# A shared accumulator tile of two banks is closed and made anew as two tiles of one bank each

## The chip, the cores and the metric

The kernel runs on one core of one Trainium2 chip. The metric is device time in microseconds of one execution, as a median of runs. TensorE (PE) multiplies, with its weight loads listed as PEld; VectorE (DVE), ScalarE (ACT) and GpSimd (POOL) do the elementwise work; SyncE (SP) issues the transfers. Products are summed in PSUM, eight banks of 512 fp32 numbers per partition, from which DVE and ACT read them.

## The reference, cut to what matters

Linear attention with positive random features, 8 batches of 8 heads, 576 tokens, head width 64, 128 features, and behind it a two-layer network on 4608 tokens of width 512, hidden width 2048:

```python
def phi(x):
    h = x @ omega.T - sum(x * x) / 2
    return exp(h - max(h)) / sqrt(m)
q_p, k_p = phi(q * scale), phi(k * scale)
kv, z = k_p.T @ v, sum(k_p)
x = (q_p @ kv) / (q_p @ z + 1e-06)          # heads side by side: 4608 x 512
h = x @ w_in                                 # 512 -> 2048
out = maximum(0.01 * h, h) @ w_out           # 2048 -> 512
```

## The kernel before

Nearly every operand is split into two fp16 parts, and a product is three passes of matmuls (high by high, high by low, low by high). The tokens go through in nine blocks of 512 (`NB`), counted by `j`. For each block `query_block` makes the attention's output (features by the matmuls of line 609, numerators by those of lines 899 to 901) and `feed_forward` applies the two layers. `key_batch` makes the keys' sums. For the first two blocks `first_layer` (line 1048) does the first layer in plain products. From block 2 on (`FIRST_FAST`), `fast_first_layer` takes a Strassen-like scheme of seven products in place of eight (line 1102), whose partial sums are read out of PSUM and combined by ACT and DVE. The second layer is plain (line 1284) up to block 6, and by seven products (line 1209) from block 7 on (`TAIL`).

The class `Plan` collects all operations with estimated durations, walks through them with a greedy list scheduler, and emits them in the order found; each engine's queue then holds that order. The order is fixed when the program is built, and on the chip an engine only waits for semaphores. A recording layer under the kernel adds these semaphore waits from who reads and who writes each tile.

PSUM's eight banks are given out as `pj` (two banks, for projections), `pj0` (two banks, a second one for the first phase), `ffn` (three tiles of a bank) and `mi` (one bank), in line 298. `pj0` is needed by class `Whole` alone, for the first two key batches and the first query block (line 688). Afterwards its halves serve as the places 3 and 4 of the kind `ffn`: lines 306 to 309 append two views of the one tile to `tiles["ffn"]`, and `over` tells the planner that they come free only when every buffer of the kind `pj0` has been used up. So from then on a buffer of the kind `ffn` may lie in one of three tiles of its own, or in either half of a fourth tile of two banks. The function `at` (line 369) maps a planned buffer to its tile. In the profile a name such as `pj<-xt,w` at line 1102, 1048, 1284 or 1209 is one of these halves; `pj` at line 609 is the projection's own tile.

In `four_tiles` the buffers `a`, `c` and `d` of a quadrant are such places (lines 1148 to 1171): `product(a, ...)` fills `a`, `so_far(a)` reads it by ACT or DVE (line 360 is the helper behind it), `product(d, ...)` fills another, `add(u1, d)` reads it by DVE (line 1118), and then `product(a, "S2", ...)` goes on adding into `a`, for which it has to wait until `so_far(a)` has read it. In the plain first layer each result is read by an ACT activation (line 1057), in the plain second layer by line 360.

In the built program before, waits on `pj0` are by the whole tile: a read of one half waits for the last matmul that stands ahead of it in the planned order into either half, and a matmul into one half waits for the reads of both.

Of the kernel before, what the change touches and what calls it, by code (L numbers as in the profile page):

```python
# [8 lines left out]
F32 = mybir.dt.float32  # L9
# [6 lines left out]
PSUM = bass.MemoryType.PSUM  # L16

P = 128
# [248 lines left out]
def performer_ffn(ctx: ExitStack, tc, qT, kT, qn, kn, vn, omT, eye, w_in, w_out, out):  # L267
# [3 lines left out]
    ps = ctx.enter_context(tc.tile_pool(name="ps", bufs=1, space=PSUM))  # L271
# [26 lines left out]
    banks = {"pj": (1, 1024), "pj0": (1, 1024), "ffn": (3, 512), "mi": (1, 512)}  # L298
    tiles = {k: [sb.tile(shape, dt, tag=f"{k}{i}", name=f"{k}_{i}") for i in range(n)]
             for k, (n, shape, dt) in kinds.items()}  # L300
    for k, (n, size) in banks.items():
        tiles[k] = [ps.tile([P, size], F32, tag=f"{k}{i}", name=f"{k}_{i}") for i in range(n)]
    scratch = tiles["mi"][0][:, 384:]


    over = {}
    for i in range(2):
        over["ffn", len(tiles["ffn"])] = [("pj0", 0)]
        tiles["ffn"].append(tiles["pj0"][0][:, 512 * i:512 * i + 512])
    late = tiles["v1"][0].rearrange("p g e -> p (g e)")  # L310
    half = HP * VT * E
    tiles["vr"] = [late[:, :half].rearrange("p (g e) -> p g e", e=E)]
# [54 lines left out]
                     for e, c, g in (("POOL", pool_(n), nc.gpsimd), ("DVE", stt(n), nc.vector)) if e in engines], **of)  # L367

    def at(b):
        return tiles[b.kind][b.place]  # L370

    def flat(a):
# [38 lines left out]

    whole = buf("xt")
    om32 = lambda: at(whole).rearrange("p i c t -> p (i c t)").bitcast(F32)[:, :2 * M]
    minus_half = lambda: at(whole).rearrange("p i c t -> p (i c t)").bitcast(F32)[:, 2 * M:4 * M]

    def omega():
# [29 lines left out]
    class Weight:  # L446
# [12 lines left out]
        def load(self, i, prio):  # L459
            w, b = self.w, buf("big")  # L460
            self.raws[i] = b

            def run():
                raw = at(b).bitcast(U32)
                if self.name == "w1":
                    k, s = i % 4, i // 4
                    nc.sync.dma_start(out=raw, in_=w[k * P:(k + 1) * P, 2048 * s:2048 * (s + 1)])
                else:
                    nc.sync.dma_start(out=raw.rearrange("p (f e) -> p f e", e=2 * DM),
                                      in_=w[2 * i * P:2 * (i + 1) * P, :].rearrange("(f p) x -> p f x", p=P))  # L470
            op("SP", 0.45, run, w=[b], prio=prio, moved=1 << 20)
# [915 lines left out]
```

## Time and profile before

| | us |
|---|---|
| median of 3 runs | 942.38 |
| lowest and highest run | 939.09 and 943.46 |
| the profiled execution: its own time | 938.46 |
| the profiled execution: span of its instructions | 936.7 |
| PE busy | 886.2 (95%) |
| DVE busy | 752.0 (80%) |
| ACT busy | 606.9 (65%) |
| POOL busy | 326.5 (35%) |

The span is the time from the first to the last instruction of the profiled execution; 1.8 us of its own time lie around it. Up to about 140 us weights are converted and the first attention blocks made; from then on matmuls of the network and of the attention alternate on PE. A matmul's duration in the profile is longer than the distance to the next, since they are pipelined: matmuls of 256 columns that take 273 ns follow each other every 109 ns, those of 512 columns that take 379 ns every 216 ns.

### The profile page before, as it was taken

The numbers are of one execution on the slowest core, as the hardware profiler recorded it, in microseconds if no ns is written. First come the engines' busy times: TensorE is split into PE (matmuls) and PEld (weight loads), VectorE is DVE, ScalarE is ACT, GpSimd is POOL, SyncE is SP. The second block draws the span as 40 slices with busy tenths as digits, with TensorE's granted clock in tenths as the row PEclk, the third lists the DMA queues.
The fourth block names the chain that finished last, engine by engine and source line by source line (L and its number), as shares of the span: only waits on it lengthen the run. The fifth ranks groups of instructions, "written<-read, shape, count | busy, mean of one in ns | idle before, by whom it ended". The sixth has DMA issues, their size and how long they took to land.

```text
span 936.7 us, 20382 instructions
## 1 busy us (share of the span) xinstructions
PE 886.2 (95%) x8102; PEld 633.8 (68%) x8102; DVE 752.0 (80%) x1384; ACT 606.9 (65%) x905; POOL 326.5 (35%) x290
## 2 busy tenths in 40 slices
PE   4786999999999799999999999999999999998998
PEld 3774566555455685588557855786579657887887
DVE  7999788988888689887778887877988788992861
ACT  5786795567665587578756864686568555653741
POOL 2333637567745344125211531172115222210010
PEclk7897999999999999999999999999999999999999
DMA  9798236975489998788789997888698886632401
GB/s 366 282 258 252 56 60 136 238 191 120 94 187 274 275 236 195 188 210 244 156 183 243 233 219 187 203 236 181 115 237 215 196 158 162 178 77 88 135 1 45
DMA packets 279103, 171.17 MB, mean 183 GB/s; under 512 B 195296, under 2 KB 242144, under 8 KB 277984
## 3 DMA queue, kind: packets, MB, share of 16 engines
q1 hardware_dynamic: 279008, 169.87, 71.9%
q8 instruction: 63, 1.03, 0.5%
q14 instruction: 32, 0.26, 0.1%
HBM read 105.87 MB, written 16.78 MB: 131 GB/s over the span
## 4 chain that ended last, share of the span: by engine, by line
PE 82%; DVE 8%; DMA 4%; ACT 3%; issue 2%; SPq 1%; DVEq 0%; ACTq 0%
PE ffn L1284 16%; PE ffn L1102 14%; PE pj L1284 12%; PE pj L1102 10%; PE ffn L1048 6%; PE pj L609 5%; PE ffn L1209 5%; PE pj L1209 3%; PE pj L688 2%; PE pj L1048 2%; DMA xt<-xn 1%; DMA t<-z 1%; PE mi L899 1%; DVE wt L487 1%; PE mi L806 1%
## 5 line engine op out<-in xcount | busy, mean ns | idle before, releaser
L1102 PEld LDWEIGHTS <-w 128*128 128x128 f16 x2352 | 228.4, 98 | 42.2 <-issue 11.5
L366 POOL TENSOR_TENSOR big<-row,big 128x512 f16<-128x512 f32 x116 | 148.5, 1292 | 272.5 <-ACT big L360 261.8
L1284 PEld LDWEIGHTS <-big 128*128 128x128 f16 x1344 | 127.3, 98 | 136.3
L1284 PE MATMUL ffn<-wt,big 128*128 128x512 f16 x816 | 190.2, 379 | 0.0
L1102 PE MATMUL ffn<-xt,w 128*128 128x256 f16 x1044 | 140.8, 274 | 3.3 <-DMA xt<-xn 3.1
L1284 PE MATMUL pj<-wt,big 128*128 128x512 f16 x528 | 124.1, 379 | 0.0
L640 ACT ACTIVATE p<-p,little 128x1024 f32<-128x1024 f32 x68 | 70.0, 1029 | 52.9 <-DVE p L637 52.9
L617 DVE TENSOR_REDUCE st<-pj 128x8 f32<-128x1024 f32 x68 | 73.1, 1075 | 25.7 <-PE pj L609 25.4
L1102 PE MATMUL pj<-xt,w 128*128 128x256 f16 x660 | 93.1, 273 | 0.5 <-ACT row L360 0.5
L1048 PE MATMUL ffn<-xt,w 128*128 128x512 f16 x312 | 73.6, 387 | 8.3 <-DMA xt<-xn 7.9
L360 ACT ACTIVATE big<-row 128x512 f16<-128x512 f32 x128 | 77.1, 621 | 3.0 <-DVE row L1074 2.3
L366 DVE TENSOR_TENSOR ph<-p,ph 128x1024 f16<-128x1024 f32 x56 | 72.6, 1296 | 6.8 <-ACT ph L360 6.6
L637 DVE SCALAR_TENSOR_TENSOR p<-pj,sc,st 128x1024 f32<-128x1024 f32 x68 | 77.1, 1134 | 0.7
L569 ACT ACTIVATE z<-nat 128x512 f32<-128x512 f32 (+1 forms) x56 | 36.3, 648 | 55.2 <-DMA t<-z 44.8
L1048 PEld LDWEIGHTS <-w 128*128 128x128 f16 x384 | 37.0, 99 | 50.6 <-issue 11.7
L609 PE MATMUL pj<-om,t 128*128 128x128 f16 x944 | 64.0, 219 | 4.2 <-DMA t<-z 2.4
L609 PEld LDWEIGHTS <-t 128*128 128x128 f16 x944 | 57.7, 98 | 14.6 <-DMA t<-z 3.7
L1102 PE MATMUL ffn<-w,w 128*128 128x256 f16 x360 | 58.9, 272 | 1.7 <-ACT z L1229 1.7
L360 ACT ACTIVATE ph<-p 128x1024 f16<-128x1024 f32 x56 | 58.8, 1050 | 0.7
L366 POOL TENSOR_TENSOR v<-xp,v 128x768 f16<-128x768 f32 (+1 forms) x15 | 26.5, 1768 | 86.5 <-ACT v L360 86.4
L571 DVE TENSOR_REDUCE sq<-z 128x8 f32<-128x512 f32 (+1 forms) x56 | 39.6, 708 | 18.5 <-ACT z L569 18.4
L1125 ACT ACTIVATE row<-row 128x512 f32<-128x512 f32 x71 | 43.8, 623 | 14.2 <-DVE row L1118 13.8
(236 smaller groups left out, 1804.5 us busy)
## 6 DMA issues: line engine op xcount, KB each, us to landing
w<-w1d SPq DMA_DIRECT2D x196, 256.0 KB, 3.3
v<-vn SPq DMA_DIRECT2D x28, 650.0 KB, 4.8
big<-w_in SPq DMA_DIRECT2D x8, 1024.0 KB, 9.8
big<-w_out SPq DMA_DIRECT2D x8, 1024.0 KB, 6.0
nat<-qn SPq DMA_DIRECT2D x32, 256.0 KB, 3.7
out<-row SPq DMA_DIRECT2D x32, 256.0 KB, 2.7
w1d<-wt SPq DMA_DIRECT2D x16, 256.0 KB, 3.2
nat<-kn SPq DMA_DIRECT2D x12, 320.0 KB, 3.8
```

Of the source, the lines that this page charges most:

```text
L360: ("ACT", act(n, int(pointer)), lambda: nc.scalar.activation(dst(), src(), AF.Copy, scale=1.0 if scale is None else value()), False),
L366: return ways([(e, c, lambda g=g: g.tensor_tensor(dst(), a(), b(), op=ALU.subtract), True) for e, c, g in (("POOL", pool_(n), nc.gpsimd), ...
L571: op("DVE", dve(n), lambda: nc.vector.tensor_reduce(at(self.sq)[:, :2 * nt], square().rearrange("p (g d) -> p g d", d=D), axis=AX.X, op=AL ...
L609: nc.tensor.matmul(at(pj)[:, 512 * h + c * M:512 * h + (c + 1) * M], at(self.t)[:, 2 * (c0 + c) + h, :], om[:, w, :], start=(w == 0), stop ...
L617: op("DVE", dve(n * M), lambda: nc.vector.tensor_reduce(row(0), pv(), axis=AX.X, op=ALU.max), r=[pj], w=[st], prio=prio)
L637: op("DVE", dve(n * M), lambda: nc.vector.scalar_tensor_tensor(p(), pv(), down(), row(2).rearrange("p (g o) -> p g o", o=1).broadcast_to([ ...
L640: op("ACT", act(n * M, 1), lambda: nc.scalar.activation(flat(p()), flat(p()), AF.Exp, bias=shift), w=[p32], r=["ones"], prio=prio)
L1048: nc.tensor.matmul(at(ph), wk[wp][:, c:c + P], xt[:, 512 * xp:512 * xp + 512], start=(i == 0), stop=(i == 3 * KT - 1))
L1102: nc.tensor.matmul(pair(bank)[:, f], wt[:, k, wp, f * P:f * P + P], operand(xname, k, xp), start=(first and f == k == i == 0), stop=(k == ...
L1125: op("ACT", act(512), lambda: nc.scalar.activation(at(g), at(src), AF.Prelu, scale=H_DOWN * (TAIL_DOWN if tail else 1.0), alpha=0.01), r=[ ...
L1209: nc.tensor.matmul(pair(bank)[:, t], g()[:, gp, f, t * P:t * P + P], operand(wname, 2 * q + f, wp), start=(first and q == t == f == i == 0 ...
L1284: nc.tensor.matmul(at(po), g_(q)[:, s, gp, t * P:(t + 1) * P], wf[wp], start=(q == s == 0 and gp == wp), stop=(q == s == 3 and gp == 1))
```

## The change

`pj0` is taken from a pool of its own. The two extra places of the kind `ffn` stay empty at first. The first time that `at` is asked for one of them, while the planned order is being emitted, that pool is closed, which gives its two banks back, and a new pool with two tiles of one bank each is opened there; the places now hold these. The planner gets the same kinds, places and rules.

```diff
+    first = ExitStack()
     for k, (n, size) in banks.items():
-        tiles[k] = [ps.tile([P, size], F32, tag=f"{k}{i}", name=f"{k}_{i}") for i in range(n)]
+        pool = first.enter_context(tc.tile_pool(name="ps0", bufs=1, space=PSUM)) if k == "pj0" else ps
+        tiles[k] = [pool.tile([P, size], F32, tag=f"{k}{i}", name=f"{k}_{i}") for i in range(n)]
...
         over["ffn", len(tiles["ffn"])] = [("pj0", 0)]
-        tiles["ffn"].append(tiles["pj0"][0][:, 512 * i:512 * i + 512])
+        tiles["ffn"].append(None)
+
+    def two_banks():
+
+        first.close()
+        ps2 = ctx.enter_context(tc.tile_pool(name="ps2", bufs=1, space=PSUM))
+        for i, place in enumerate(p for p, tile_ in enumerate(tiles["ffn"]) if tile_ is None):
+            tiles["ffn"][place] = ps2.tile([P, 512], F32, tag=f"late{i}", name=f"late_{i}")
...
     def at(b):
+        if tiles[b.kind][b.place] is None:
+            two_banks()
         return tiles[b.kind][b.place]
```

Each engine's queue holds the same instructions with the same shapes in the same order as before. Of the 1788 matmuls that went into a half of `pj0` after 140 us, each now goes into a tile `late_0` or `late_1`. The tiles lie in other banks than before (`pj0` was in banks 2 and 3 and its successors are in 6 and 7; `ffn` moved from 4 to 6 to 2 to 4, and `mi` from 7 to 5). What differs besides is the waits. Of the 108 reads by ACT and DVE out of the former halves, 34 wait for an earlier matmul than before, 6 to 84 matmuls earlier in PE's order, and three name one 12 matmuls later, a matmul that an earlier wait of the other reader used to stand for. On PE some 60 waits of matmuls for ACT or DVE fall away, name an earlier read, or move to a matmul further on. There is one new wait: the first matmul into `late_0` (at 143.29 us in the trace before) waits for PE's own 574th matmul, the last of line 688 into `pj0` (118.41 us). POOL's and SP's queues have the same waits.

## Rows read from the trace of the kernel before

**Rows 1.** The page: busy time by engine, then the chain that ended last, shares by engine.
```profile
PE 886.2 (95%) x8102; PEld 633.8 (68%) x8102; DVE 752.0 (80%) x1384; ACT 606.9 (65%) x905; POOL 326.5 (35%) x290
...
PE 82%; DVE 8%; DMA 4%; ACT 3%; issue 2%; SPq 1%; DVEq 0%; ACTq 0%
```

**Rows 2.** Waits of PE, 140 to 937: who waited for whom, total us, times, longest.
```profile
PE pj L1102 <- ACT row L360: 3.4, 6, 0.7
PE ffn L1102 <- DMA xt<-xn: 3.1, 1, 3.1
PE pj L609 <- DMA t<-z: 2.4, 2, 1.9
PE mi L901 <- DMA qp<-ph: 2.2, 1, 2.2
```

**Rows 3.** Timeline, 419 to 449: start, us, engine, line, operation, count, [idle before <-releaser].
```profile
421.91 0.49 PE L1102 MATMUL pj<-xt,w 128*128 128x256 f16 x3
422.50 0.60 ACT L360 ACTIVATE row<-pj 128x512 f32<-128x512 f32 x1 [1.82 <-PE pj L1102]
...
423.15 0.49 PE L1102 MATMUL pj<-w,w 128*128 128x256 f16 x3 [0.74 <-ACT row L360]
...
443.23 0.60 ACT L360 ACTIVATE row<-pj 128x512 f32<-128x512 f32 x1 [1.14 <-PE pj L1284]
...
443.88 0.49 PE L1102 MATMUL pj<-w,w 128*128 128x256 f16 x3 [0.74 <-ACT row L360]
...
447.61 0.49 PE L1102 MATMUL pj<-w,w 128*128 128x256 f16 x3 [0.75 <-ACT row L360]
```

**Rows 4.** Timeline, six later places where PE restarts, and one reader.
```profile
501.84 0.49 PE L1102 MATMUL ffn<-xt,w 128*128 128x256 f16 x3 [0.15 <-ACT row L360]
...
606.34 0.92 PE L1102 MATMUL pj<-xt,w 128*128 128x256 f16 x7 [0.32 <-ACT row L360]
...
696.57 0.60 PE L1102 MATMUL pj<-xt,w 128*128 128x256 f16 x4 [0.18 <-ACT row L360]
...
794.59 0.49 PE L1102 MATMUL pj<-w,w 128*128 128x256 f16 x3 [0.21 <-DVE z L1118]
...
803.51 0.49 PE L1102 MATMUL pj<-w,w 128*128 128x256 f16 x3 [0.89 <-DVE row L1118]
...
860.60 0.60 ACT L360 ACTIVATE row<-pj 128x512 f32<-128x512 f32 x1 [2.95 <-PE pj L1209]
861.25 0.49 PE L1102 MATMUL pj<-w,w 128*128 128x256 f16 x3 [0.69 <-ACT row L360]
```

**Rows 5.** Timeline, 233 to 270: a chain through three engines, and a read like its first.
```profile
233.88 2.75 PE L1048 MATMUL pj<-xt,w 128*128 128x512 f16 x12
...
236.67 0.60 ACT L1057 ACTIVATE row<-pj 128x512 f32<-128x512 f32 x1 [1.81 <-PE pj L1048]
...
238.48 0.69 DVE L571 TENSOR_REDUCE sq<-z 128x8 f32<-128x512 f32 x1 [1.00 <-ACT z L569]
...
249.61 0.38 PE L609 MATMUL pj<-om,t 128*128 128x128 f16 x4 [1.75 <-DVE p L637]
...
269.56 0.69 ACT L360 ACTIVATE row<-pj,s 128x512 f32<-128x512 f32 x1 [3.92 <-PE pj L1284]
```

**Rows 6.** The chain in order of time, 200 to 330: one transfer, start, us.
```profile
285.96 7.74 DMA t<-z
```

**Rows 7.** Busy us by stretch: PE, PEld, DVE, ACT, POOL, then PEclk, DMA share, GB/s.
```profile
275.00:300.00 25.00, 23.07 (x189) 12.39 (x188) 23.32 (x41) 12.76 (x17) 14.10 (x13) 1.00 0.98 266
322.70:326.10 3.40, 3.40 (x20) 2.48 (x18) 2.83 (x3) 2.95 (x4) 1.39 (x2) 0.50 0.79 264
420.00:450.00 30.00, 27.76 (x299) 23.57 (x298) 21.34 (x43) 23.55 (x41) 17.25 (x14) 1.00 0.83 226
780.00:803.00 23.00, 22.40 (x209) 18.60 (x207) 21.55 (x34) 15.36 (x27) 7.20 (x4) 1.00 0.60 164
```

**Rows 8.** The page, DMA issues: count, KB each, median us from issue to landing.
```profile
t<-z SPq DMA_TRANSPOSE x56, 3.5
```

## The prediction

> **What bounds the kernel now.** I read the page first: PE is busy for 95% of the span, and 82% of the chain that ended last runs through it [rows 1]. Then the view of waits, from 140 us on, where the change acts. PE waits there for little, and the four rows that I keep are most of it: 3.4 us for ACT reads of a half of the shared tile, in six places, and 3.1 + 2.4 + 2.2 = 7.7 us for transfers [rows 2]. So PE sets the end. A gain counts only if it takes a stall out of PE's queue, and it can hardly be more than the stalls that are there. The timeline then shows what a stall costs and who ends it. At 421.91 PE starts its last three matmuls into one half of the tile. ACT has been idle for 1.82 us and begins to read the other half only at 422.50, when these matmuls are through; PE goes on at 423.15, when ACT has read [rows 3]. The half that ACT reads was complete before, since 12 matmuls into the other half, at a pitch of 0.109 us, stand in between. So the two halves take turns here though they are two banks.
>
> The Trainium skill, Perfetto Trace Analysis, section Matmuls, says that independent matmul groups should rotate through different PSUM banks, so that ACT or DVE read one while the next group runs. By that rule alone the kernel before has what the change brings and the sum would be nothing; the row at 422.50 disagrees, since its read waits 1.82 us although the banks differ.
>
> **What one stall costs.** The idle time that the view prints is counted from the modelled end of the last matmul, and understates it. At 421.91 the three matmuls start at 421.91, 422.02 and 422.13; the next would start at 422.24 and starts at 423.15, so 0.91 us are lost where the view prints 0.74. The difference of about 0.16 is the duration of 0.27 less the pitch of 0.11; for 512 columns it is 0.379 less 0.216, the same. I add 0.16 to each printed idle time.
>
> **The change part by part.** The order on all engines stays, so no instruction and no transfer is added. The new wait of PE for its own 574th matmul is 25 us late (118.41 against 143.29) and costs nothing; a few extra semaphore instructions on ACT and DVE stand in place of others that go. The other banks have no price in any row; I take 0. What is left is the waits.
>
> *Three places at 423, 444 and 448.* ACT's read no longer waits for the other half. At 422.50 ACT could have read 1.82 us earlier: read done at about 421.3, PE wants the half at 422.24, cover 0.95 us. At 443.23 ACT was idle for 1.14, so the read ends at about 442.7 and PE wants it at about 443.0: cover 0.3 us. The third is like it [rows 3]. All three stalls go whole: 0.90 + 0.90 + 0.91 = 2.7 us. If ACT were busier there, as after PE has moved, up to 0.6 each could come back; that is the lower bound, 0.9 us.
>
> *606, 697 and 861.* The same figure: 0.32 + 0.16 = 0.48, 0.18 + 0.16 = 0.34, 0.69 + 0.16 = 0.85 [rows 4]. At 860.60 ACT had been idle for 2.95 us, so its read has room. Sum 1.7 us, bounds 0.8 and 1.7.
>
> *502.* PE waits for a read of another tile that stands in ACT's queue behind a read of a half: 0.15 + 0.16 = 0.3 us [rows 4], bounds 0 and 0.3, and I take 0.2, since another matmul's wait comes close behind.
>
> *795 and 804.* The matmul at 794.59 waits for a DVE read of the other half and loses 0.37 us [rows 4]; this wait goes. But at 803.51 PE waits for DVE's read of its own half, which stays, and DVE is busy for 21.55 of the 23 us ahead of it [rows 7]. A PE that comes 0.37 earlier waits 0.37 longer. I take 0 for the pair.
>
> *250.* From 233.88 twelve matmuls, six into one half and six into the other, and ACT reads the first six only at 236.67 after an idle time of 1.81. With the change it may read six pitches of 0.216, so 1.3 us, earlier. Behind it in ACT's queue stands the square for which DVE sits idle 1.00 us, and DVE is then gapless up to the operation for which PE waits at 249.61, printed as 1.75 [rows 5]. DVE's idle time is the cap: 1.0 us, bounds 0 and 1.0.
>
> *294.* The same figure recurs at 269.56, where ACT reads a half after 3.92 us of idle time [rows 5] and may do so up to 1.3 us earlier. What it makes later goes by transposes, the last of which, `t<-z` at 285.96, ends a wait of PE that is at most 1.9 long [rows 2, 6]. So 1.3 is the upper bound. But this transfer takes 7.74 us, where the median of its kind is 3.5 [rows 6, 8], and the engines that move data are busy 0.98 from 275 to 300 [rows 7], so how much of an earlier issue becomes an earlier landing is open: between 0 and 1.3 I take 0.4, nearer to nothing.
>
> Sum: 2.7 + 1.7 + 0.2 + 0 + 1.0 + 0.4 = 6.0 us. The end follows PE one to one, since only two DVE reads and the last store come behind it. Against the profiled execution's own 938.46 this gives 932.5. The median of the runs shown is 942.38, 3.9 us above that execution, and nothing in the change depends on what sets them apart, so I take the 6.0 from the median: **936.4 us**, 0.64% less. Bounds of the sum: low ends 0.9 + 0.8 + 0 + 0 + 0 + 0 = 1.7; high ends 2.7 + 1.7 + 0.3 + 0.4 + 1.0 + 1.3 = 7.4, to which stalls of 0.1 to 0.2 that I left out add up to 1 us.
>
> **The rivals.** *The gain is caught later.* PE comes earlier to waits that are not fed by PE. For: the transfer of 7.7 us stands in a stretch where data movement is full [rows 6, 7], and the stretch of DVE up to 803 is nearly so. Against: the full stretch lies ahead of 423, where most of the gain arises, and a PE ahead of time also feeds ACT and DVE earlier. If the terms at 250 and 294 are lost and the three large places return their lower bound, 0.9 + 1.7 + 0.2 = 2.8 remain: 939.6 us.
>
> *The clock.* At 322.7 the granted clock falls to 0.50, the lower of the two levels (1.2 GHz), for 3.4 us, after PE had stalled once for `xt<-xn` (3.1 us, line 1102) and once for `qp<-ph` (2.2 us, line 901) [rows 2, 7]. Half the rate for 3.4 us costs 1.7 us. If the shift lets this fall away, the time is 936.4 - 1.7 = 934.7; if PE's longer waits for the same transfers bring a second one, 938.1. The Trainium skill, TensorE: Matmul & The Clock Gate, section A second HAM failure mode: psum-queue depth-cycling, says that short idle times between matmul groups, when PSUM banks are cycled, throttle the clock again. By that rule the three stalls at 423 to 448 would cost clock as well, and removing them would give that back on top; the trace disagrees, with 1.00 granted throughout 420 to 450.
>
> *Nothing happens*, as by the page's rule on banks above: 942.4 us. The row at 422.50 speaks against it, and so do the waits in the built programs.
>
> *Slower: transfers collide.* The loads `w<-w1d` of line 1092 go out when PE has done with a place in the ring, so a PE that is ahead sends them earlier, into the queue ahead of transposes for which PE has no time to spare. A transpose then lands after 7.7 instead of 3.5 us, 4.2 later [rows 6, 8]. The place is 450 to 750, behind a stretch with a share of 0.83 already [rows 7]. Two of these cost 8.4 - 6.0 = 2.4 us net; from three on the kernel is measurably slower, 942.4 + 12.6 - 6.0 = 949.0 us. Against it: SP's queue keeps its order, and both the loads and the transposes move with PE.
>
> **How the numbers follow.** Forecast, a gain of 4.7 to 8 us: 0.66. The clock's extra gain, 934.7: 0.07. Caught later, 939.6: 0.19. Nothing: 0.03. Collision, 949.0: 0.05. About 0.5%, or 4.7 us, is what a measurement of this kernel can tell from no change, so faster is 0.66 + 0.07 = 0.73, same 0.19 + 0.03 = 0.22, slower 0.05. The range should leave out 2 in 10: it reaches from a gain of about 11 (the high end of 7.4, the small stalls, the clock, and the 1.5 us or so by which a median of three moves, from 939.09 to 943.46) to a gain of 1.5 (near the low end of the sum): 931.5 to 940.9.
>
> **What would show it.** In the changed kernel's timeline PE should run through at the three places of [rows 3] with the usual pitch, and ACT's read there should be released by matmuls of its own product, a microsecond or more ahead of PE's return. The six waits for ACT of [rows 2] should fall from 3.4 to below 0.5 us. PE's wait for DVE near 249 should shrink from 1.75 to about 0.8. The wait at 803.51 should stay or grow a little. The prediction is wrong if PE's total of waits for transfers rises by what the others fall, if a second stretch at the lower clock appears, or if ACT's reads turn out to be late for other reasons.

## The result: 932.8 us, 0.9% less

The kernel before took 941.12 us (939.09 to 943.46, four runs), the changed kernel 932.77 us (931.76 to 934.21, four runs). The ratio is 0.9912 with an interval of 0.9882 to 0.9941, so 8.35 us less, of which the interval allows 5.6 to 11.1. The prediction, 936.4 us with a range of 931.5 to 940.9, held the time; it asked for 6.0 us. The profiled execution of the changed kernel took 934.21 us, with a span of 932.4.

In the changed kernel's listing a line of the body is 11 higher than before (1102 is now 1113, 1284 is 1295), the helper that records ACT's reads is line 369 (was 360), and the two tiles are called `late` where the halves were `pj`. First the page of the changed kernel: busy time by engine, then the shares of the chain that ended last. They answer to [rows 1].

```profile
PE 886.1 (95%) x8102; PEld 636.3 (68%) x8102; DVE 751.1 (81%) x1384; ACT 608.9 (65%) x905; POOL 326.6 (35%) x290
...
PE 79%; DVE 11%; DMA 5%; issue 1%; ACT 1%; SPq 1%; DVEq 0%; ACTq 0%
```

Instructions and busy time are what they were: 8102 matmuls in 886.1 us against 886.2. The change did no work less; it can only have taken waiting away. ACT's share of the chain went from 3% to 1%, PE's from 82% to 79%; DVE's rose from 8% to 11% and that of transfers from 4% to 5%.

The waits of PE from 140 to 937 us (who waited for whom, total us, times, longest), all of them, against [rows 2]:

```profile
PE ffn L1113 <- DMA xt<-xn: 3.3, 1, 3.3
PE mi L912 <- DMA qp<-ph: 2.6, 2, 2.1
PE pj L620 <- DMA t<-z: 2.4, 2, 2.1
PE ffn L1113 <- ACT z L1240: 1.7, 1, 1.7
PE late L1113 <- DVE row L1129: 1.3, 1, 1.3
PE pj L620 <- DVE p L648: 0.6, 1, 0.6
PE ffn L1220 <- DVE row L1252: 0.2, 1, 0.2
```

The row of six waits for ACT, 3.4 us in all, is gone, and nothing has taken its place: the three rows of transfers add up to 8.3 us where they were 7.7. The wait for DVE's `p` fell to 0.6, and the one for DVE's `row` rose to 1.3; both were named in advance.

The timeline of the changed kernel around the first three places (start, us, engine, line, operation, count), against [rows 3]:

```profile
421.80 0.58 ACT L369 ACTIVATE row<-late 128x512 f32<-128x512 f32 x1
...
423.60 0.49 PE L1113 MATMUL late<-w,w 128*128 128x256 f16 x3
...
441.10 0.58 ACT L369 ACTIVATE row<-late 128x512 f32<-128x512 f32 x1
...
442.06 1.46 PE L1295 MATMUL late<-wt,big 128*128 128x512 f16 x6
...
443.36 0.49 PE L1113 MATMUL late<-w,w 128*128 128x256 f16 x3
...
444.89 1.46 PE L1295 MATMUL late<-wt,big 128*128 128x512 f16 x6
444.96 0.58 ACT L369 ACTIVATE row<-late 128x512 f32<-128x512 f32 x1
...
446.19 0.49 PE L1113 MATMUL late<-w,w 128*128 128x256 f16 x3
```

None of these rows has an idle time in brackets. ACT's read at 441.10 is over at 441.68, before PE even begins the product into the other tile at 442.06, where before it began at the end of that product. The six matmuls of 442.06 at a pitch of 0.216 end their places in the queue at 443.36, which is exactly where the next row starts; 444.89 + 1.30 = 446.19 likewise. At 444.96 ACT reads one tile while PE fills the other, and the read takes 0.58 us, as long as the others: reading beside the filling costs nothing that a row shows.

The granted clock and the load of that stretch, changed kernel (PE, PEld, DVE, ACT, POOL busy, then PEclk, DMA share, GB/s), against the row of the same window in [rows 7]:

```profile
420.00:450.00 30.00, 30.00 (x320) 25.57 (x318) 23.94 (x47) 26.88 (x47) 21.18 (x16) 1.00 0.95 244
```

PE now fills the whole 30 us, at a clock of 1.00 (2.4 GHz) as before.

**Place by place.** To see where the gain arises I took the start of the same matmul in both traces and followed the shift between them, set to zero at the first matmul into one of the late places (143.29 us before, 147.27 in the changed kernel). Ahead of it the two are one program, and there the traces differ by 4 us for another reason, told at the end. In the table a minus is time gained between two marks, given by the time in the trace of before. The second column of times is a second trace of the changed kernel, from the run `e5_again` below.

| from to (before) | forecast | first trace | second trace |
|---|---|---|---|
| 245 to 260 | -1.0 | -1.15 | -1.14 |
| 300 to 345 | | -1.98 | +1.11 |
| 345 to 400 | | -0.28 | -0.28 |
| 400 to 449 | -2.7 | -2.82 | -2.81 |
| 500 to 530 | -0.2 | -0.69 | -0.69 |
| 580 to 620 | -0.48 | -0.66 | -0.47 |
| 620 to 690 | | -0.11 | -0.11 |
| 690 to 720 | -0.34 | -0.36 | -0.36 |
| 720 to 760 | | -0.15 | +1.49 |
| 760 to 797, 797 to 806 | 0 as a pair | -0.38, +0.37 | -0.38, +0.37 |
| 850 to 870 | -0.85 | -0.85 | -0.85 |

The places with a forecast give 6.5 and 6.3 us, where the forecast for them was 5.6 (the 6.0 without the 0.4 for 294). From the first late matmul to the end the first trace gains 8.2 us, the second only 3.3; what parts them is mostly the rows of 300 to 345 and of 720 to 760. The first of these is taken up under the clock, the second under the rivals.

### The profile page after: what moved, and what is told of

It reads as the page before. It is cut to its first block, busy times and chain, and to the rows that moved or that the text cites. A ratio compares the mean times of both kernels' runs of the same rounds, so it can differ in the third digit from the quotient of the medians.

```text
span 932.4 us, 20377 instructions
## 1 busy us (share of the span) xinstructions
PE 886.1 (95%) x8102; PEld 636.3 (68%) x8102; DVE 751.1 (81%) x1384; ACT 608.9 (65%) x905; POOL 326.6 (35%) x290
## 4 chain that ended last, share of the span: by engine, by line
PE 79%; DVE 11%; DMA 5%; issue 1%; ACT 1%; SPq 1%; DVEq 0%; ACTq 0%
PE ffn L1295 15%; PE ffn L1113 15%; PE late L1295 11%; PE late L1113 10%; PE ffn L1059 5%; PE pj L620 5%; PE ffn L1220 5%; PE late L1220 3%; PE pj L699 2%; PE mi L817 2%; DMA qp<-ph 1%; DMA t<-z 1%; DMA xt<-xn 1%; DVE wt L498 1%; PE mi L910 1%
## 5 line engine op out<-in xcount | busy, mean ns | idle before, releaser
L1295 PE MATMUL late<-wt,big 128*128 128x512 f16 x528 | 124.1, 379 | 0.0
L1113 PE MATMUL late<-xt,w 128*128 128x256 f16 x660 | 92.8, 273 | 0.0
L582 DVE TENSOR_REDUCE sq<-z 128x8 f32<-128x512 f32 (+1 forms) x56 | 39.5, 706 | 18.2 <-ACT z L580 18.1
L1136 ACT ACTIVATE row<-row 128x512 f32<-128x512 f32 x71 | 43.8, 624 | 11.3 <-DVE row L1129 11.1
```

The lines of the kernel that those rows point to most:

```text
L582: op("DVE", dve(n), lambda: nc.vector.tensor_reduce(at(self.sq)[:, :2 * nt], square().rearrange("p (g d) -> p g d", d=D), axis=AX.X, op=AL ...
L1113: nc.tensor.matmul(pair(bank)[:, f], wt[:, k, wp, f * P:f * P + P], operand(xname, k, xp), start=(first and f == k == i == 0), stop=(k == ...
L1136: op("ACT", act(512), lambda: nc.scalar.activation(at(g), at(src), AF.Prelu, scale=H_DOWN * (TAIL_DOWN if tail else 1.0), alpha=0.01), r=[ ...
L1295: nc.tensor.matmul(at(po), g_(q)[:, s, gp, t * P:(t + 1) * P], wf[wp], start=(q == s == 0 and gp == wp), stop=(q == s == 3 and gp == 1))
```

## Experiments

All times are compared with the kernel before on the same chip. The ratio is not formed from the two medians printed beside it and can differ from theirs by up to 0.15%; microseconds gained or lost are by the ratio where nothing else is said.

### Other banks, and the closing of the tile, without the split

The first edit keeps all that the change does but the split: the tile is closed, and one tile of two banks is made anew, used half by half.

```
-        for i, place in enumerate(p for p, tile_ in enumerate(tiles["ffn"]) if tile_ is None):
-            tiles["ffn"][place] = ps2.tile([P, 512], F32, tag=f"late{i}", name=f"late_{i}")
+        both = ps2.tile([P, 1024], F32, tag="late", name="late_0")
+        for i in range(2):
+            tiles["ffn"][3 + i] = both[:, 512 * i:512 * i + 512]
```

> The first tile is closed and a new one opened in the same banks as in the changed kernel, but it is again one tile of two banks with two views. Its waits are those of the kernel before but for the one wait of PE for itself. Theory (the waits by the whole tile are the whole cost): no gain, 941 us within 2, PE waits for ACT reads of a half again some 3.4 us in six places. Rival (other banks, or closing the tile, bring the gain): about 933 us.

It took 939.73 us against 940.63, a ratio of 0.999 (0.997 to 1.001). Two rows of its waits of PE:

```profile
PE late L1114 <- ACT row L370: 3.4, 6, 0.7
...
PE pj L621 <- DVE p L649: 1.8, 1, 1.8
```

Both are those of the kernel before, to the tenth (six waits for ACT's reads with 3.4 us in all, and 1.8 us for DVE's `p`). The banks, the pool that is closed, the wait of PE at 143 us bring and cost nothing that can be measured (the interval reaches from 2.8 us less to 0.9 us more); the gain is in the split alone. And since the two halves of this tile are two banks, it isn't the bank that makes PE and ACT wait for each other here, but the tile.

### The change in two parts, by time

With a few lines more the two places can change from a shared tile to two of their own at any point of the program. `e2_late` leaves them shared up to about 300 us and apart after; `e3_early` does the opposite (`apart = [1, 0]`).

```
+    apart, now = [0, 1], [-1, first]
+    def two_banks(i):
+        now[1].close()
+        now[0], now[1] = i, ExitStack()
+        ps2 = now[1].enter_context(tc.tile_pool(name=f"ps2_{i}", bufs=1, space=PSUM))
+        if apart[i]:
+            tiles["ffn"][3:] = [ps2.tile([P, 512], F32, tag=f"late{i}{k}", name=f"late_{k}") for k in range(2)]
+        else:
+            both = ps2.tile([P, 1024], F32, tag=f"late{i}", name="late_0")
+            tiles["ffn"][3:] = [both[:, 512 * k:512 * k + 512] for k in range(2)]
...
+            i = sum(b.turn >= turn for turn in [50])
```

> Two tiles only from the first block of the fast first layer on (about 300 us); until then the new tile is one of two banks. Theory: the term at 250 is lost (0.95 us), the rest stays, so 933.7 us; PE's wait for DVE near 250 is 1.8 us again, the waits for ACT after 420 are gone. Rival (the early shift also removes the stretch at the lower clock near 323): 1.5 us more lost, 935.2 us, and the stretch is back in the trace.

> The other way round: two tiles up to about 300 us, then one of two banks again. Theory: a gain of 1.0 us, 940.1 us; PE's wait for DVE near 250 is 0.6 to 0.8 us, the six waits for ACT are back. Rival (the early shift removes the stretch at the lower clock): a gain of 2.5 us, 938.6 us, with no such stretch in the trace.

Apart late, the time was 933.15 us against 940.63, a ratio of 0.9934 (0.9904 to 0.9965), which is 6.2 us less (7.5 by the medians). Apart early, it was 938.68 us, a ratio of 0.9981 (0.9959 to 1.0004), 1.8 us less with an interval that touches no change. The two add up to 8.0 us, the whole change's 8.35. Of the waits of PE in `e2_late`:

```profile
PE pj L628 <- DVE p L656: 1.8, 1, 1.8
...
PE late L1121 <- DVE row L1137: 1.3, 1, 1.3
```

And of those in `e3_early`:

```profile
PE late L1121 <- ACT row L374: 3.4, 6, 0.7
...
PE pj L628 <- DVE p L656: 0.6, 1, 0.6
```

The two mechanisms separate cleanly. The early part alone takes the wait for `p` near 250 from 1.8 to 0.6 and leaves the six waits for ACT; the late part alone removes the six, and raises the wait at 803 to 1.3, but leaves the wait for `p`. That is the chain of [rows 5] confirmed, from ACT's read over DVE's idle time to PE. In the shift of the same matmul `e3_early` gains 1.14 us from 245 to 260 and nothing from 400 to 449; `e2_late` nothing and 2.81.

Each of the two also had a rival, by which the early part brings gain through the clock. Neither is settled. In `e2_late` the stretch at the lower clock is back, as its rival said (0.50 from 325.5 to 328.9 us, and once more at 298.2), but the median is nearer to the theory's 933.7 us than to the 935.2 that the rival asked for. In `e3_early` the time is the rival's 938.6 us to a tenth, but the trace has such a stretch, which the rival excluded (0.51 from 310.8 to 314.2 us). The interval of each run holds both of its numbers.

### A window around the three large places

The same code with three stretches, shared, apart, shared (`apart = [0, 1, 0]`), was to price the three stalls of [rows 3] by themselves. The first try began the middle stretch at `turn` 74.

> Two tiles only from about 418 to 461 us; before and after that one tile of two banks. Theory: the three stalls at 423, 444 and 448 go whole and nothing gives them back, so a gain of 2.8 us, 937.8 us (ratio 0.997), with PE gaining 2.8 us between 400 and 449 in the trace and holding it to the end. Rival (a PE that is ahead meets waits that do not move with it): the 2.8 us shrink by 620 or 850 in the trace, and the median is that of before, 940.6.

It took 940.19 us against 942.22, a ratio of 0.9979 (0.9958 to 0.9999), less than expected, and its timeline says why:

```profile
426.26 0.60 ACT L374 ACTIVATE row<-late 128x512 f32<-128x512 f32 x1 [1.96 <-PE late L1121]
...
426.91 0.49 PE L1121 MATMUL late<-w,w 128*128 128x256 f16 x3 [0.74 <-ACT row L374]
```

This is the stall of 423, unchanged: the stretch began just behind it. The other two went, worth 1.81 us between 425 and 449. So I began the window earlier:

```
-            i = sum(b.turn >= turn for turn in [74, 80])
+            i = sum(b.turn >= turn for turn in [65, 80])
```

> Two tiles only for the buffers from the 65th to the 79th of the kind ffn, so that the stretch covers all three places at 423, 444 and 448; the window before this one began just behind the first of them. Theory: PE gains 0.9 us between 400 and 425 and 1.85 between 425 and 449, 2.75 in all, against the traces in which the tile is shared, and the waits for ACT reads fall from six to three. The median is 2.75 us below before, ratio 0.997 within 0.002. Rival (the first place needs more than its own buffers): 1.8 us between 400 and 449, as in the narrower window.

Now all three went: 0.94 us from 400 to 425 and 1.87 from 425 to 449, together 2.81, where the forecast said 2.7. The time was 939.89 us against 943.20, a ratio of 0.9967 (0.9948 to 0.9986), so 3.1 us less (3.3 by the medians); the interval holds 2.8. The waits of PE keep what lies outside the window, the three at 606, 697 and 861:

```profile
PE late L1121 <- ACT row L374: 1.2, 3, 0.7
PE mi L918 <- DVE xp L938: 1.1, 1, 1.1
...
PE late L1121 <- ACT row L1144: 0.7, 1, 0.7
```

The second and the third row were not there before. In this execution's trace the 2.8 us are given back later: 0.7 between 500 and 530, 0.8 between 580 and 690, 2.0 between 720 and 760. The median kept the gain; how many executions lose it in this way, one trace doesn't say.

The third row stands at 639 us and is one more shared turn. Of the other traces that share the tile there, `e1_joint`, `e3_early` and `e6_window` lose 0.49, 0.25 and 0.86 us at this matmul against the trace of before, `e7_double` loses nothing, and those with two tiles there gain 0.11. So the traced execution of before has fewer of these stalls than some others with a shared tile, and a gain measured against it is on the small side.

### The other pair made to share

If a shared tile is the cause, putting two other places (1 and 2 of the same kind) into one tile of two banks must cost time. Once in the changed kernel:

```
-    banks = {"pj": (1, 1024), "pj0": (1, 1024), "ffn": (3, 512), "mi": (1, 512)}
+    banks = {"pj": (1, 1024), "pj0": (1, 1024), "ffn": (1, 512), "fj": (1, 1024), "mi": (1, 512)}
...
+    both = tiles.pop("fj")[0]
+    tiles["ffn"] += [both[:, 512 * i:512 * i + 512] for i in range(2)]
```

> The two late tiles stay apart, but two of the three other tiles of the kind ffn (places 1 and 2, which hold 77 buffers where the late two hold 54) become one tile of two banks. Theory: sharing costs wherever it is, by its use: 8.35 x 77/54 = 11.9 us, so about 944.7 us, bounds 939 to 952, with PE waiting for ACT or DVE reads of the other half at ffn. Rival (what counts is only that the late places are apart): about 933 us.

And once, by the same lines, in the kernel before, so that both pairs share:

> The kernel before, in which besides the late places also places 1 and 2 of the kind ffn lie in one tile of two banks. Theory (each shared pair has its price): the 18 us between the changed kernel and the one with places 1 and 2 shared come on top of before, 958.8 us, bounds 951 to 967. Rival (stalls of the two pairs fall together): under 951 us.

The first took 950.99 us, a ratio of 1.0103 (1.0071 to 1.0134) to the kernel before; against the 932.77 of the changed kernel in its own runs the pair costs 18.2 us (18.0 by the two ratios). The second took 958.19 us, a ratio of 1.0164 (1.0132 to 1.0196), 15.5 us over the kernel before and where it was expected. The size of the first was expected too small, 12 us where it was 18. This pair is used in the first 143 us too, where the late places don't exist: the first matmul into those starts at 150.16 us in `e4_swap` and at 150.60 in `e7_double`, but at 143 to 148 in the other traces. Some waits of PE in `e7_double`:

```profile
PE pj L1104 <- ACT row L362: 3.4, 6, 0.7
...
PE fj L1104 <- ACT row L362: 1.4, 2, 0.7
PE fj L1104 <- DVE row L1120: 1.0, 2, 0.8
...
PE fj L1104 <- ACT z L362: 0.7, 1, 0.7
```

`fj` is the new shared tile. Its waits for ACT have the 0.7 us of the old ones, and the six old ones stand unchanged beside them. The mechanism can be switched on at will in places that never had it. Its whole price there was not followed: the rows of `fj` that wait for ACT or DVE add up to 6.4 us of the 15.5, the first 143 us take some more, and in this execution the clock falls to 0.50 a second time, at 597.9 us.

### The changed kernel once more

> The changed kernel once more, for a narrower ratio and a second trace. Theory: 932.6 us, ratio 0.9912 within 0.003. In the trace from 143 us on, PE gains 1.1 us between 245 and 260, 2.8 us between 400 and 449, 0.85 us near 861, as in the first trace; what it gains between 300 and 345 is left to the clock and differs. Rival (part of the gain was luck of the first runs): ratio 0.994 or above.

It took 934.94 us (932.13 to 936.38) against 942.22, a ratio of 0.9910 (0.9882 to 0.9938), which is 8.5 us less (7.3 by the medians). What it was for is the clock. After its first trace the changed kernel seemed to have got rid of the stretch at the lower clock that [rows 7] shows at 322.7. Two windows, first of the changed kernel's first trace, then of `e1_joint`, which has all the waits of the kernel before:

```profile
320.00:345.00 25.00, 22.86 (x260) 20.45 (x258) 22.25 (x43) 20.71 (x36) 9.94 (x8) 1.00 1.05 275
```

```profile
320.00:345.00 25.00, 24.44 (x279) 22.00 (x280) 21.07 (x39) 19.97 (x35) 11.60 (x10) 1.00 0.99 263
```

Both have 1.00 throughout, with the change and without the split. And `e5_again`, the changed kernel, has it back:

```profile
323.80:327.20 3.40, 3.40 (x18) 2.34 (x17) 2.76 (x4) 2.39 (x3) 1.01 (x1) 0.51 0.77 257
```

For 3.4 us the granted clock is 0.51, the lower level of 1.2 GHz. So the stretch comes and goes from one execution to the next, whichever of the two kernels it is. Of all ten traces three have none between 140 and 900 us (the changed kernel's first, `e1_joint`, `e6_window`), and the others have one or two. The 1.66 us that the first trace gained between 322 and 330 (as `e1_joint` did) are the price that the prediction gave for half the rate over 3.4 us, 1.7, but they are not the change's.

## Why the prediction was right, step by step

- **What bounds the kernel, and what a stall costs.** Right. The gain came out of PE's queue, at stalls that can be pointed to, and printed idle time + 0.16 was their price: 0.90, 0.90 and 0.91 forecast at 423, 444 and 448; 0.94, 0.90 and 0.90 measured.
- **423, 444, 448.** 2.7 forecast, 2.82, 2.81, 2.81 and 2.81 in the two traces of the changed kernel, in `e2_late` and in `e8_wide`; 0.06 of this lies at 432. The lower bound of 0.9 wasn't needed, though ACT was busy, as it feared: the three reads have no idle time ahead of them, so what they wait for now is ACT's own work and not, as the prediction had it, the matmuls of their own product. They still end 1.2, 1.7 and 0.65 us before PE comes back; a microsecond or more was forecast for each.
- **606, 697, 861.** 0.48, 0.34 and 0.85 forecast; 0.47 to 0.66, 0.36 and 0.85.
- **502, and the small stalls.** A term that was mis-sized. I took 0.2 for 502; it gave 0.32, its upper bound. Small stalls that I had left out of the sum gave 0.8 us in both traces of the changed kernel, and none of it in `e1_joint`: 0.28 between 345 and 400, 0.06 at 432, 0.24 at 510, 0.11 at 638, 0.12 at 722. (A gain of 0.12 at 526, which makes up the 0.69 of 500 to 530, is not the split's: `e1_joint` and `e3_early` have it too.) The prediction allowed up to 1 us for such stalls in its range, and 0 in its sum; they should have stood in the sum.
- **795 and 804.** Right, and the clearest case of a gain that is no gain: 0.38 won, 0.37 given back. The changed kernel's timeline at the second of them, against 803.51 in [rows 4]:

```profile
799.37 0.68 DVE L1129 TENSOR_TENSOR row<-late,row 128x512 f32<-128x512 f32 x1
...
800.11 0.49 PE L1113 MATMUL late<-w,w 128*128 128x256 f16 x3 [1.27 <-DVE row L1129]
```

PE waits 1.27 where it waited 0.89: it comes 0.38 earlier to a DVE that was busy before and is no earlier.

- **250.** 1.0 forecast, 1.15 and 1.14 measured. Four rows of the changed kernel's timeline, against [rows 5], show the step that I took for the cap:

```profile
239.98 0.60 ACT L1068 ACTIVATE row<-late 128x512 f32<-128x512 f32 x1 [0.52 <-PE late L1059]
...
241.91 0.18 DVE L928 RECIPROCAL r<-r 128x4 f32<-128x4 f32 x1
242.01 0.66 DVE L582 TENSOR_REDUCE sq<-z 128x8 f32<-128x512 f32 x1
...
253.07 0.38 PE L620 MATMUL pj<-om,t 128*128 128x128 f16 x4 [0.60 <-DVE p L648]
```

The twelve matmuls start at 238.49 here, so ACT reads 1.49 us behind their start instead of 2.79; the 1.3 us are the six pitches. DVE's idle 1.00 ahead of line 582 is gone, and PE's wait went from 1.75 to 0.60. The cap was read a little too low, in the way in which PE's stalls would have been without the 0.16. Line 582 starts 0.10 us behind the start of the operation ahead of it here; before, that operation was

```profile
237.31 0.18 DVE L917 RECIPROCAL r<-r 128x4 f32<-128x4 f32 x1
```

and the next started 1.17 behind it, at 238.48. So the gap that is printed as 1.00 was worth 1.07. The rest of the 1.15 came along DVE's row of operations behind it, two of which took 0.03 us less each.
- **294.** The other term that was mis-sized: 0.4 in the sum, and no gain in either trace. PE's wait for the transpose there, 1.93 before, is 2.13 and 2.30 in the two traces of the changed kernel, so PE loses 0.20 and 0.38 us at this matmul. `e1_joint`, which shares the tile, gains 0.46 there, and `e3_early`, which has two tiles up to about 300 us, gains 0.44. Executions differ here by more than the term, so its true size stays open.
- **Rivals.** *Caught later* is real in single executions: of five traces with two or all three of the large places apart (the two of the changed kernel, `e2_late`, `e6_window`, `e8_wide`), four lose 0.7 to 2.0 us between 720 and 760 (`e5_again` waits 1.5 there for a transpose, `e8_wide` for DVE), and only the first trace of the changed kernel loses nothing. The trace of before, `e1_joint` and `e3_early` lose nothing there either, so this may follow from PE being ahead; `e7_double`, which is not ahead, loses 0.5. The medians keep the gain. *The clock* fell away in the first trace, which is what that rival said, but as shown not through the change. The prediction set the Trainium skill, TensorE: Matmul & The Clock Gate, section A second HAM failure mode: psum-queue depth-cycling, against the trace at the three stalls; by that rule their removal would have given back clock as well. No run here shows it: the clock was 1.00 there before, and 400 to 449 gained what the stalls alone cost. *Nothing happens* is refuted by the result. What it rested on, that two banks are enough, is refuted by `e1_joint`: it has the rotation between banks that the Trainium skill asks for in Perfetto Trace Analysis, section Matmuls, and it gained nothing, where two tiles gained 8.35 us. *Colliding transfers*: PE's waits for transfers were 8.3 us in the first trace, against 7.7, but 11.2 in the second:

```profile
PE pj L620 <- DMA t<-z: 4.2, 3, 2.3
PE mi L912 <- DMA qp<-ph: 3.8, 3, 2.9
PE ffn L1113 <- DMA xt<-xn: 3.2, 1, 3.2
```

The transpose that PE waits for at 732.82 landed 5.00 us after its issue there; the same transpose took 3.2 to 3.6 in the other nine traces. This is a sign that the prediction named against itself, seen in one execution, which at 936.38 us was still shorter than the shortest of before on that chip, 937.36; the runs as a whole don't bear the rival out.
- **The size.** The forecast was 6.0 us, its places give 6.3 to 6.5 in two traces, with the small stalls about 7, and the runs say 8.35 (5.6 to 11.1) and 8.5 (5.8 to 11.1). That 6.0 comes so close to what its places gave is in part luck: the 0.4 for 294 stands in for some of the 0.8 left out. Between 7 and 8.5 nothing is left to explain that the intervals don't cover. The traced execution of before, 938.46 us, lies below its medians of 940.6 to 943.2, and the two of the changed kernel, 934.21 and 936.38, are the longest of their runs, so these traces are more likely to show too little than too much. Of the 3.6 us between the forecast time, 936.4, and the measured one, 1.3 come from the median of before, 941.12 now and 942.38 when it was forecast.

What was not tried is to separate the two directions of a shared tile, ACT's read held back by PE's writes, and PE's write held back by ACT's read.

## What to carry to other kernels

Two places that take turns must be two tiles, not two views of one: on the path of a full engine a shared turn cost 0.1 to 0.9 us here, and the order needn't change for it to go. Price such stalls one at a time from the timeline, printed idle time plus the difference between duration and pitch, count the small ones too, and look behind each for the next wait on an engine without idle time, which takes its gain back. Follow the same instruction through two traces before you trust a difference of spans.

## What the runs showed that I had not expected

The same first 143 us, with the same instructions, took 143.13 us in `e1_joint` and 148.26 in `e3_early`. This is as large as the effect under study, and a trace that starts with 4 us more, as that of the changed kernel does, hides half the gain: the spans differ by 936.7 - 932.4 = 4.3 us, the shift since the first late matmul is 8.2, of which the 2.0 between 300 and 345 are not the change's. The granted clock in the first 140 us is 0.88 before and 0.87 in the changed kernel, made up of several stretches at 0.50 (1.2 GHz). The time of the first late matmul goes with where they lie. The trace of before, `e1_joint`, `e5_again` and `e8_wide` have a clock of 0.50 from 15 to 32 us and 0.95 to 1.00 from 32 to 50, and get there at 143.1 to 144.7 us; the changed kernel's first trace, `e3_early` and `e6_window` have 0.63 to 0.66 and then 0.72, and get there at 147.3 to 148.3. I didn't find what places them.

The stretch near 323 us has the waits of [rows 2] for transfers ahead of it, 3.1 and 2.2 us, and came in the kernel before and in `e5_again`, but not in the first trace of the changed kernel and not in `e1_joint`, where the same waits were 3.2 and 2.1. The waits alone don't decide it.
